# Random-feature attention into a gated MLP on one core: later planned DMA landings, a new set of plan seeds, and other places for the tails' x and P1

## The chip, the cores and the metric

The kernel runs on one core of one Trainium2 chip. The metric is the device time of one execution in microseconds (us), lower is better. The program is one launch; the host only lays the inputs out in another order. In the profile PE is TensorE's matmuls and PEld its weight loads, DVE is VectorE, ACT is ScalarE, POOL is GpSimd, and SP is SyncE, which here does nothing but issue DMAs.

## The reference

```python
def _attn_ref(q, k, v, omega):               # q, k, v: (8, 8, 576, 64), omega: (128, 64)
    scale = 1.0 / np.sqrt(np.sqrt(D))
    def phi(x):                              # of q * scale, k * scale
        proj = np.einsum('bhsd,md->bhsm', x, omega)
        h = proj - np.sum(x * x, axis=-1, keepdims=True) / 2.0
        return np.exp(h - np.max(h, axis=-1, keepdims=True)) / np.sqrt(m)
    kv = np.einsum('bhsm,bhsd->bhmd', k_p, v)
    z = np.sum(k_p, axis=2)
    num = np.einsum('bhsm,bhmd->bhsd', q_p, kv)
    den = np.einsum('bhsm,bhm->bhs', q_p, z)[..., None] + 1e-06
    return num / den
def _moe_ref(x, w_a, w_b, w_out):            # x: (4608, 512); 512 -> 1536 -> 512
    return ((x @ w_a) * (x @ w_b)) @ w_out
```

The attention's output, heads side by side, is the x of the gated product. The q that is passed in is 3.366 times as large as the 0.1 of k and v. Weights arrive as 64-bit floats.

## The kernel before, in words

**Stages.** A *unit* u is a batch with a pair of heads, 32 in all (8 batches, 4 pairs). Attention of a unit: random features of k and q by one burst of TensorE, row maxima and biases on VectorE, exponentials on ScalarE, sums of k's features (z) on GpSimd and VectorE, k times v on TensorE, division by the denominators, a turn of q's features through DRAM, and the product that gives x. The 576 rows of a batch are 512 and a *tail* of 64; the tails of all batches are gathered in DRAM (xtd) and form a ninth batch of 512 rows, b = 8. The MLP runs over batches b = 0 to 8 in steps; `steps` holds the first matmul of each, 12 per batch. Every matmul of the MLP is made of three, with both operands split into a high and a low part.

**Seven products for eight.** Batches 0 and 1 (`moe_block`) multiply plainly. From batch 2 on (`moe_block7`) the products with w_a and w_b take a Strassen-like scheme: seven products per pair i of feature blocks and per weight w (0 is w_a, 1 is w_b), with sums of the weights (tiles t and bq) that are computed once, by `weight_sums`, stored in DRAM and loaded again for each batch. Batches 7 and 8 (`Out7`) do the same with w_out: `out_sums` makes the sums (tiles owr and otf, result ot). Of its seven products, P1 is computed into the bank p1 that the w_a and w_b products also use (`one` in `items`), and is copied by ScalarE the first time, later added by VectorE, into an oc tile. `ones7` is the list of P1 products that wait for their place in `unit`.

**Slots.** A tile lives in a slot of its ring (x0 to x3, raw0, raw1, and so on), or in one of the slots of other rings that its `more` list names. Tiles of the weight sums (wr, tf), outputs before their store (osb), and w_out's sums (owr) all use raw0 and raw1. The `LATE` lists name what the last two batches may take over from the attention.

**The planner.** The whole kernel is first recorded as a graph of operations, each with a cost in ns for the engines that can do it. `plan` simulates it: at each step every engine takes the operation that can start first, ties by priority. VectorE, ScalarE and GpSimd (`EDF`) go by due times instead, which `dues` works out backwards from TensorE's order of a first pass. The order thus found is then written out, and the engines keep it, whatever really happens: an operation that waits holds up everything behind it on its engine. DMAs are costed as their bytes at 330 bytes per ns, one after another, plus `LANDING`; a reader that is sensitive to late data has a `margin` or a `land` in addition. `slot_free` says from when a slot can be taken: the end of its last user and 70 ns (`LAT`).

`CHOSEN` holds one seed per slice of `STEP` ns. A seed other than 0 makes `shifted` add Gaussian noise to the due times of the operations due within `LOOK` of the slice's start. The kernel before has one tuple of 53 seeds and slices of 20,000 ns.

**Lines.** L417, L419 and L425 are the copies and differences that split into high and low parts. L428 is the issue of every DMA except those named apart. L594 and L611 are the attention's bursts, L651 and L652 the biases, L834 and L835 `groups`, L844 and L845 `total`, L889 and L890 `inv`. L884 is the denominators' row sum, L1073 the plain product with w_out, L1089 to L1096 `out_sums`, L1143 a product of `Out7`, L1263 and L1271 the plain MLP, L1294 to L1303 `weight_sums`, L1356 and L1366 a product of seven and the sum behind it, L1416 the gate's product.

Of the kernel before, what the change touches and what calls it, by code (L numbers as in the profile page):

```python
# [39 lines left out]

CFG = dict(PORT=0.5, EDF=("DVE", "ACT", "POOL"), ROUNDS=2, STEP=20000, LOOK=60000, TRIES=8, NOISE=(1000,), CHOSEN=((4,6,0,1,0,7,8,6,1,5,0,0,1,8,0,2,0,0,0,8,1,0,0,0,0,6,1,0,0,6,7,3,2,0,0,4,0,0,0,0,0,1,3,2,0,1,0,0,0,0,0,0,0),), TOOK=[], SAY=False, ZS=800, ZB=(1500, 3000, 5000), ZD=(1500, 3000, 4500), HQ=(2500, 4000, 5000), BACK2=(1500, 2500, 4000), TW=(), WAIT=150, RAW=2000, FAST=(0, 1, 2, 3), JOIN0=False, WARM=8, HROOM=["w0", "u1", "w1", "u2", "w2", "u3"], H=3, TURN=(7,), BACK=1500, AT=2, GATES=(-4, -1, 2, 5), SQPE=4, MARGIN=1200, LOAD=2500, SUMS=1000, NATS=(1, 2, 3), CONV=(28000, 2600))

# [16 lines left out]
class Graph:  # L59
    LAT = 70  # L60
    OVER = {"DVE": 78, "ACT": 100, "POOL": 40, "PE": 0, "SP": 0}
    ENGINES = ("PE", "ACT", "DVE", "POOL", "SP")
    BW, LANDING = 330.0, 2000

# [74 lines left out]
    def dues(self):  # L139
# [21 lines left out]
        while heap:  # L161
            d, _, o = heapq.heappop(heap)
            e = next(iter(o.eng))
            cost = o.end - o.start if o.bytes else o.eng[e]
            if e in CFG["EDF"]:
                now = min(-d, ptr.get(e, inf))
                if now < -d:
                    heapq.heappush(heap, (-now, -o.n, o))
                    continue
                ptr[e] = now - max(30, o.eng[e] - self.OVER[e])  # L170
            o.due = -d
            for n in before[o]:
                same = "PE" in o.eng and "PE" in n.eng
                late[n] = min(late[n], o.due - cost - o.margin - (0 if same else self.LAT + (150 if "PE" in n.eng else 0)))
# [52 lines left out]
    def run(self, until=1e12, due=None):  # L227

        free, ready, found = self.free, self.ready, {}
        while len(self.done) < len(self.ops):  # L230
            best = None
            for e in self.ENGINES:
                mine = None
                for o in ready[e]:
                    at = 0, ()
                    if o.alloc:
# [5 lines left out]
                        if not at or at[1] == ():  # L242
                            continue
                    s = max(free[e], o.need, at[0])
                    for x in o.eng:
                        if x != e and max(free[x], o.need, at[0]) + o.eng[x] <= s + o.eng[e] - (o.eng[e] <= o.eng[x]):
                            break
# [43 lines left out]

    def cost(self, since):

        at, c = since, 0
        for o in self.done:
            if "PE" in o.eng and o.end > since:
                gap = max(0, o.start - at)
                c += gap + 1600 * (gap > 1900)
                at = o.end
        return c  # L300

    def shifted(self, due, at, k):

        rnd = random.Random(k)
        near = [o.n for o in self.ops if o.end is None and o.due < at + CFG["LOOK"]]
        due = list(due)
        for n in near:
            due[n] += rnd.gauss(0, CFG["NOISE"][k % len(CFG["NOISE"])])
        return due

    def plan(self):

        self.begin()
        self.run()
        self.sort()
        self.dues()
        due, best, chosen = [o.due for o in self.ops], None, CFG["CHOSEN"]
        for turn in range(len(chosen) or CFG["ROUNDS"]):
            self.begin()
            at, now, took = 0, list(due), []  # L320
            while len(self.done) < len(self.ops):
                i = len(took)
                seeds = [chosen[turn][i]] if chosen else [0] + [1 + 1000 * turn + k for k in range(CFG["TRIES"])]
                if len(seeds) > 1:
                    kept, tried = self.keep(), []
                    for k in seeds:
                        self.run(at + CFG["LOOK"], self.shifted(now, at, k) if k else now)
                        tried.append((self.cost(at), k))
                        self.back(kept)
                    seeds = [min(tried)[1]]  # L330
                took.append(seeds[0])
                now = self.shifted(now, at, seeds[0]) if seeds[0] else now
                at += CFG["STEP"]
                self.run(at, now)
            self.sort()
            end = max(o.end for o in self.order)
            if chosen or best is None or end < best[0]:
                best = end, self.order, {o: (o.start, o.end, o.eng, [b.slot for b in o.alloc]) for o in self.ops}
                due = now
                CFG["TOOK"].append(took)  # L340
            if CFG["SAY"]:
                print(turn, end, flush=True)
        _, self.order, was = best
        for o in self.ops:
            o.start, o.end, o.eng, slots = was[o]
            for b, slot in zip(o.alloc, slots):
                b.slot = slot
        return self.order
# [28 lines left out]
def tile_attention_moe(ctx: ExitStack, tc: tile.TileContext, kqt, kqtt, kqn, kqnt, vx, omst, idn, wab, wout, out):  # L377
# [12 lines left out]
    for name, n in dict(X=2, Xw=0, nat=2, x2=0, v=2, hk=1, hq=2, qd=1, kvz=0, sm=3, sq=3, ht=3, Xt=1, xl=0, xts=2, rd=2, x=4, xa=2, xf=2, Sa=2, Sb=2, st=0,  # L390
# [6 lines left out]

    LATE = dict(wo=["hk0", "hq0"], ot=["X0", "X1", "hq1", "qd0"], owr=["raw0", "raw1"], og=["nat0", "nat1", "ht0", "ht1"], ogf=["xf0", "xf1"],
                oc=["v0", "v1", "Xt0", "raw0", "raw1"])
# [218 lines left out]
    def scores(nm, b, pri, x, xdep, dst, c0, sm, sq, flat, held, more):  # L618
# [29 lines left out]
        def biases(e):  # L648
# [3 lines left out]
            nc.vector.scalar_tensor_tensor(bi, s, -1.0, tm, op0=ALU.mult, op1=ALU.subtract)  # L652
        g.op({"DVE": 300}, biases, r=[(sm, (c0, 0)), (sm, (c0, 1)), (psq if sq is None else sq, None)], w=[(sm, (c0, 0)), (sm, (c0, 1))], prio=pri + 2)
        for w in range(2):
# [6 lines left out]
    ends = {}  # L661
    xstage = {}

    def pair(u, gate):
# [143 lines left out]
    def z_sums(u, pr, hk, mg):  # L808
# [27 lines left out]
        g.op({"DVE": 2 * dve(2 * M)}, groups, r=[(zs, None)], w=[(z2, None), (zq, 0)], alloc=[zq], prio=pri, margin=CFG["ZS"])  # L836

# [5 lines left out]
        def total(e):  # L843
            nc.vector.tensor_reduce(zw.ap[0:32, 0:8], zq.ap[0:32, 0:4].rearrange("p i c -> p c i"), axis=X, op=ALU.add)  # L844
            nc.vector.transpose(zx.ap[0:32], zw.ap[0:32])  # L845
        g.op({"DVE": 320}, total, r=[(zq, 0), (zq, 1)], w=[(zw, None), (zx, None)], alloc=[zx], prio=pri)
        g.op({"SP": 330}, dma(lambda: zd, lambda: zx.ap[0:8]), r=[(zx, None)], w=[(zd_b, None)], prio=-30, nbytes=32 * 8 * 4)
# [27 lines left out]
    def divide(u, pr, hq, zb):  # L875
# [15 lines left out]
        g.op({"DVE": 340}, inv, r=[(dn, None)], w=[(dn, None)], prio=pri)  # L891
        for c in range(NCH):
# [87 lines left out]
    def tok_tail(b, hp, nm, pr, mg, more, vb, h, xt):  # L980
# [47 lines left out]
        g.op({"PE": 4 * 108}, go, r=[(x32t, None), (ident, None)], w=[(px, None)], alloc=[px, *xt.new], prio=pr + 150, margin=mg)  # L1028
        split(b, hp, lambda: px.ap[:], (px, None), pr + 150)
# [54 lines left out]
    def out_sums(i, wo, ot, gate=()):  # L1084
# [3 lines left out]
        for k in range(2):  # L1088
            g.op({"DVE": dve(E)}, lambda e, k=k: nc.vector.tensor_tensor(wr.ap[:, k], f(wo[k].ap[:, 0]), f(wo[k].ap[:, 1]), op=ALU.add),  # L1089
                 r=[(wo[k], None)], w=[(wr, k)], alloc=[wr, tf] if k == 0 else [], prio=-7, deps=gate, land=2500)  # L1090
        b11, b12, b21, b22 = (lambda k=k, h=h: wr.ap[:, k, HM * h:HM * h + HM] for k in range(2) for h in range(2))
# [228 lines left out]
    def moe_block7(b):  # L1320
# [10 lines left out]
        def unit(i, w, C):  # L1331
# [120 lines left out]
    def attention(u, room=None):  # L1452

        gate = steps[-1:] if u >= 2 * NHP else []
        if u == KS:
# [15 lines left out]
    for b in range(B + 1):  # L1471
# [94 lines left out]
```

## Time and profile before

| what | value |
|---|---|
| median of three runs | 1061.02 us (1060.23 to 1061.48) |
| the profiled execution's own time | 1057.47 us |
| its span, first to last instruction | 1055.7 us |
| TensorE busy | 1039.7 us, 7806 matmuls |
| VectorE, ScalarE, GpSimd busy | 885.0, 597.3, 111.1 us |
| moved by DMA | 314.16 MB, 298 GB/s on the mean |
| DMAs issued on SP | t 168 and wo 96 of 512 KB, bq 84 of 256 KB, and others |

Durations below come from the one profiled execution. A group's row gives line, engine, operation, out<-in with buffer numbers left out, shapes, count, then busy time in us, mean ns of one, and the engine's idle time before such instructions with what ended it. A piece of the timeline gives start, length, engine, line, operation and tiles, and in brackets idle time and what ended it. Who ended a wait is inferred from semaphores.

### The profile page before, as it was taken

Reading aid. Unit: us, or ns where it says so; the run is one execution under the profiler, and the core shown is the slowest. Engines: PE = TensorE matmul, PEld = TensorE weight load, DVE = VectorE, ACT = ScalarE, POOL = GpSimd, SP = SyncE. Lnnn points to the kernel's source line nnn. Section 1 sums busy time; section 2 is a strip of 40 time slices with the busy share of each in tenths; the row PEclk is TensorE's granted clock in tenths of the full one; section 3 lists DMA queues with packets and bytes.
Section 4 is the critical chain, followed back from the end, with each engine's and each line's share of the span. In section 5 each row is a group of like instructions: output and inputs, shape, how many; then the busy total and the mean of one; then the engine's idle time right before and its main releaser. Section 6 shows DMA issues by size and latency. Waiting matters only on the chain. (4 is left out here: it accounts for less than half of the span.)

```text
span 1055.7 us, 22026 instructions
## 1 busy us (share of the span) xinstructions
PE 1039.7 (98%) x7806; PEld 915.4 (87%) x7806; DVE 885.0 (84%) x2218; ACT 597.3 (57%) x1650; POOL 111.1 (11%) x177
## 2 busy tenths in 40 slices
PE   9999999999999999999999999999999999999998
PEld 8877777777788888888888898988899898999998
DVE  6999999799988788888886978778876658998866
ACT  8998887666665655665564656564564213233211
POOL 0021111111111111111020111111110000000000
PEclk9999999999999999999999999999999999999999
DMA  9886877899899989988889888988887878899991
GB/s 354 315 249 224 308 258 248 279 356 340 267 334 350 311 300 300 334 312 296 297 291 353 299 297 290 360 290 292 272 287 261 277 255 294 317 373 341 364 310 47
DMA packets 123646, 314.16 MB, mean 298 GB/s; under 512 B 17680, under 2 KB 40976, under 8 KB 123536
## 3 DMA queue, kind: packets, MB, share of 16 engines
q1 hardware_dynamic: 122656, 312.10, 85.7%
q8 instruction: 61, 1.00, 0.4%
q10 hardware_dynamic: 880, 0.66, 0.2%
q14 instruction: 49, 0.40, 0.1%
HBM read 255.52 MB, written 57.18 MB: 296 GB/s over the span
## 5 line engine op out<-in xcount | busy, mean ns | idle before, releaser
L1366 DVE TENSOR_TENSOR c<-p,c 128x512 f32<-128x512 f32 (+1 forms) x336 | 207.4, 617 | 83.1 <-PE p L1356 70.4
L1073 PE MATMUL o<-wo,ghl 128*128 128x512 f32 x1008 | 258.7, 397 | 3.1 <-DVE ghl L425 2.2
L1073 PEld LDWEIGHTS o<-wo,ghl 128*128 128x128 f32 x1008 | 181.0, 188 | 42.7 <-DVE ghl L425 3.9
L1356 PE MATMUL p<-Sa,t 128*128 128x256 f32 x1008 | 134.9, 283 | 0.0
L1356 PEld LDWEIGHTS p<-Sa,t 128*128 128x128 f32 x1008 | 126.4, 189 | 0.4
L818 POOL TENSOR_TENSOR z<-hk 128x256 f32<-128x256 f32 x56 | 44.6, 797 | 653.6 <-ACT hk L657 417.9
L417 ACT CAST ghl<-c 128x512 fp32r<-128x512 f32 (+1 forms) x71 | 39.9, 576 | 101.3 <-DVE c L1416 90.6
L894 ACT ACTIVATE hq<-hq,dn 128x128 f32<-128x128 f32 x224 | 71.4, 393 | 29.9 <-DVE dn L890 28.3
L417 ACT COPY c<-p 128x256 f32<-128x256 f32 x84 | 31.1, 370 | 96.8 <-PE p L1356 91.7
L884 DVE CUSTOM_DVE_ANT_0 zero<-hq,zb 128x128 bf16<-128x128 f32 x224 | 76.0, 339 | 1.5 <-DMA zb<-zdr 0.5
L1263 PE MATMUL pa<-x,wa 128*128 128x512 f32 x288 | 74.6, 400 | 0.8 <-ACT a L417 0.7
L1356 PE MATMUL p<-x,t 128*128 128x256 f32 x504 | 73.8, 282 | 1.3 <-ACT oc L417 0.7
L1263 PE MATMUL pb<-x,wb 128*128 128x512 f32 x288 | 73.4, 398 | 1.3 <-DVE a L1271 1.3
L1356 PE MATMUL p<-Sb,t 128*128 128x256 f32 x504 | 74.3, 283 | 0.0
L1356 PE MATMUL p<-Sb,bq 128*128 128x256 f32 x504 | 73.8, 282 | 0.4 <-DMA bq<-bd 0.4
L1356 PEld LDWEIGHTS p<-x,wa 128*128 128x128 f32 x504 | 65.1, 188 | 6.5 <-DVE c L1366 3.9
L1356 PE MATMUL p<-x,wa 128*128 128x256 f32 x504 | 68.9, 283 | 1.6 <-DVE c L1366 1.6
L1356 PE MATMUL p<-x,wb 128*128 128x256 f32 x504 | 68.7, 282 | 0.4 <-DVE c L1366 0.2
L1356 PEld LDWEIGHTS p<-x,t 128*128 128x128 f32 x504 | 65.8, 188 | 3.2 <-DVE c L1366 1.5
L1356 PEld LDWEIGHTS p<-x,wb 128*128 128x128 f32 x504 | 65.0, 188 | 4.0 <-DVE c L1366 1.3
L1356 PEld LDWEIGHTS p<-Sb,t 128*128 128x128 f32 x504 | 66.2, 189 | 0.8 <-ACT c L417 0.4
L1356 PEld LDWEIGHTS p<-Sb,bq 128*128 128x128 f32 x504 | 65.8, 189 | 0.7 <-DMA bq<-bd 0.6
(202 smaller groups left out, 2032.4 us busy)
## 6 DMA issues: line engine op xcount, KB each, us to landing
t<-td SPq DMA_DIRECT2D x168, 512.0 KB
wo<-wod SPq DMA_DIRECT2D x96, 512.0 KB
bq<-bd SPq DMA_DIRECT2D x84, 256.0 KB
qdr<-qd SPq DMA_DIRECT2D x112, 160.0 KB
hq<-qdr SPq DMA_DIRECT2D x28, 640.0 KB
X<-in_kqt_dram SPq DMA_DIRECT2D x30, 512.0 KB
raw<-in_wab_dram SPq DMA_DIRECT2D x24, 512.0 KB
td<-ts SPq DMA_DIRECT2D x24, 512.0 KB
```

The costliest lines, as they stand in the source:

```text
L417: nc.scalar.copy(o(), i())
L818: g.op({"POOL": pool2(n)}, lambda e: nc.gpsimd.tensor_tensor(o(), a(), c(), op=ALU.add), r=r, w=w, alloc=list(al), prio=pri, deps=zload[-1 ...
L884: g.op({"DVE": 413}, lambda e, c=c, j=j, rr=rr, qc=qc: nc.vector.tensor_tensor_reduce(out=junk.ap[rr], in0=qc(), in1=zb.ap[rr, j], scale=1 ...
L894: g.op({"ACT": 392}, lambda e, c=c, src=src: nc.scalar.activation(hq.ap[:, c], src(), AF.Copy, scale=dn.ap[:, c:c + 1]), r=[sd, (dn, None) ...
L1073: nc.tensor.matmul(po.ap[:], ghl.ap[:, gi, t * P:(t + 1) * P], wo.ap[:, wi], start=(n == 0 and i == 0), stop=(n == NF - 1 and i == 2))
L1263: nc.tensor.matmul(pb.ap[:], wt.ap[:, wi, c], xs[c].at(xi), start=(c == 0 and i == 0), stop=(c == NC4 - 1 and i == 2))
L1356: nc.tensor.matmul(pb.ap[:, half], wcol(wi, c), xc(xi, c), start=n == 0, stop=n == 5)
L1366: g.op({"DVE": dve(n)}, lambda e: nc.vector.tensor_tensor(c4.ap[:, o], pb.ap[:, half], y(), op=ALU.add), r=[*((pb, k) for k in range(half. ...
```

## The change

- **Landings.** `LANDING` goes from 2000 to 3400. Margins that had covered late data shrink: `RAW` 2000 to 600, `LOAD` 2500 to 1100, w_out's `land` 2500 to 1100, `ZB`, `ZD`, `HQ`, `BACK2` by 1200 to 1400 at each stage. `SAFE`, 500, is new: it is added to the readers of a DMA that have neither `land` nor `margin`, and to the time at which a slot is free if a DMA was among its users. `dues` counts both as well.
- **Prices.** `biases` 300 to 379 ns, `groups` 60 more, `total` 320 to 423, `inv` 340 to 416.
- **Seeds.** One tuple of 70 seeds with slices of 15,000 ns. Noise is 300 ns for even seeds and 1000 for odd ones; an odd seed also holds two fifths of the attention's TensorE operations that are near back by up to `HOLD`, 1000 ns. The search for seeds is taken out of `plan`; `LOOK` stays.
- **Places.** xl, the tails' x as it comes back from DRAM, gets the slots v0, v1, Xt0 and hq0. `owr` gets its list from `CFG`.
- **Order.** With `ONE=((7, 1),)` P1 of batch 7, pair 1, is put in the unit of w = 1; all others stay at w = 0. `TG=1` gates each part of `weight_sums` one step earlier. `turned[CFG["G4"]:]` with `G4=4` gates the first unit of the second batch.

```diff
-    BW, LANDING = 330.0, 2000
+    BW, LANDING = 330.0, 3400
...
-            t = max(t, o.end + self.LAT)
+            t = max(t, o.end + self.LAT + (CFG["SAFE"] if o.bytes else 0))
...
-            t = max(t, d.start + 1, d.end + (0 if same else self.LAT + (150 if "PE" in d.eng else 0)) + (o.land if d.bytes else 0) - (900 if d in o.late else 0))
+            t = max(t, d.start + 1, d.end + (0 if same else self.LAT + (150 if "PE" in d.eng else 0)) + (o.land or CFG["SAFE"] * (not o.margin) if d.bytes else 0) - (900 if d in o.late else 0))
...
-                    s = max(free[e], o.need, at[0])
+                    need = o.need if due is None else o.need + due[len(self.ops) + o.n]
+                    s = max(free[e], need, at[0])
...
+        for o in near:
+            due[o.n] += rnd.gauss(0, CFG["NOISE"][k % len(CFG["NOISE"])])
+        if k % 2:
+            for o in near:
+                if "PE" in o.eng and 0 <= o.prio < 10 ** 6 and rnd.random() < 0.4:
+                    due[len(self.ops) + o.n] = rnd.random() * CFG["HOLD"]
...
+        for seeds in CFG["CHOSEN"]:
+            self.sort()
+            self.dues()
+            now = [o.due for o in self.ops] + [0] * len(self.ops)
+            self.begin()
+            for i, k in enumerate(seeds):
+                now = self.shifted(now, i * CFG["STEP"], k) if k else now
+                self.run((i + 1) * CFG["STEP"], now)
+            self.run(1e12, now)
...
-            if ones7 and w == 0:
+            if ones7 and w == ((b, i) in CFG['ONE']):
...
-        gate = steps[-1:] if u >= 2 * NHP else []
+        gate = steps[-1:] if u >= 2 * NHP else turned[CFG["G4"]:] if u == NHP else []
...
-                    xl = g.buf("xl", [P, SM], F32, f"xl{hp}", ["X0", "X1", "hk0", "hq0", "hq1"])
+                    xl = g.buf("xl", [P, SM], F32, f"xl{hp}", CFG["XL"])
...
-                weight_sums(k // 2, k % 2, [steps[NF * b + k]])
+                weight_sums(k // 2, k % 2, [steps[NF * b + k - CFG["TG"]]])
```

More of the change, by code (lines that the diff above doesn't have):

```diff
@@ L39 @@
 KS = NHP
-CFG = dict(PORT=0.5, EDF=("DVE", "ACT", "POOL"), ROUNDS=2, STEP=20000, LOOK=60000, TRIES=8, NOISE=(1000,), CHOSEN=((4,6,0,1,0,7,8,6,1,5,0,0,1,8,0,2,0,0,0,8,1,0,0,0,0,6,1,0,0,6,7,3,2,0,0,4,0,0,0,0,0,1,3,2,0,1,0,0,0,0,0,0,0),), TOOK=[], SAY=False, ZS=800, ZB=(1500, 3000, 5000), ZD=(1500, 3000, 4500), HQ=(2500, 4000, 5000), BACK2=(1500, 2500, 4000), TW=(), WAIT=150, RAW=2000, FAST=(0, 1, 2, 3), JOIN0=False, WARM=8, HROOM=["w0", "u1", "w1", "u2", "w2", "u3"], H=3, TURN=(7,), BACK=1500, AT=2, GATES=(-4, -1, 2, 5), SQPE=4, MARGIN=1200, LOAD=2500, SUMS=1000, NATS=(1, 2, 3), CONV=(28000, 2600))
+CFG = dict(PORT=0.5, EDF=("DVE", "ACT", "POOL"), STEP=15000, LOOK=60000, NOISE=(300, 1000), CHOSEN=((140892,0,232461,659925,412462,880754,0,848445,0,0,175606,0,728814,0,0,0,560286,0,0,0,0,0,0,0,0,0,0,0,0,0,0,0,0,0,0,0,0,0,0,0,0,0,0,0,0,0,0,0,0,0,0,0,0,0,0,0,0,0,545343,0,0,0,0,0,0,0,0,0,0,0),), ZS=800, ZB=(300, 1600, 3600), ZD=(300, 1600, 3100), HQ=(1100, 2600, 3600), BACK2=(300, 1100, 2600), TW=(), XL=["v0", "v1", "Xt0", "hq0"], OWR=["raw0", "raw1"], ONE=((7, 1),), SAFE=500, HOLD=1000, TG=1, G4=4, WAIT=150, RAW=600, FAST=(0, 1, 2, 3), JOIN0=False, WARM=8, HROOM=["w0", "u1", "w1", "u2", "w2", "u3"], H=3, TURN=(7,), BACK=1500, AT=2, GATES=(-4, -1, 2, 5), SQPE=4, MARGIN=1200, LOAD=1100, SUMS=1000, NATS=(1, 2, 3), CONV=(28000, 2600))
 class Buf:
@@ L173, in dues @@
                 same = "PE" in o.eng and "PE" in n.eng
-                late[n] = min(late[n], o.due - cost - o.margin - (0 if same else self.LAT + (150 if "PE" in n.eng else 0)))
+                late[n] = min(late[n], o.due - cost - o.margin - (o.land or CFG["SAFE"] * (not o.margin) if n.bytes else 0) - (0 if same else self.LAT + (150 if "PE" in n.eng else 0)))
                 left[n] -= 1
@@ L290, in sort @@
         self.order = sorted(self.done, key=lambda o: (o.start, o.n))
[L292 to L300, printed above, removed]
     def shifted(self, due, at, k):
         rnd = random.Random(k)
-        near = [o.n for o in self.ops if o.end is None and o.due < at + CFG["LOOK"]]
+        near = [o for o in self.ops if o.end is None and o.due < at + CFG["LOOK"]]
         due = list(due)
-        for n in near:
-            due[n] += rnd.gauss(0, CFG["NOISE"][k % len(CFG["NOISE"])])
+        for o in near:
[4 more added lines that the diff above has]
+                    due[len(self.ops) + o.n] = rnd.random() * CFG["HOLD"]
         return due
@@ L314, in plan @@
         self.run()
-        self.sort()
[L316 to L347, printed above, removed]
+        for seeds in CFG["CHOSEN"]:
[7 more added lines that the diff above has]
+            self.run(1e12, now)
+        self.sort()
         return self.order
@@ L396, in tile_attention_moe @@
                 tst=["Sa0", "Sb0", *(f"u{k}" for k in range(NF))], bq=["a0", "a1"], osb=["raw0", "raw1"])
-    LATE = dict(wo=["hk0", "hq0"], ot=["X0", "X1", "hq1", "qd0"], owr=["raw0", "raw1"], og=["nat0", "nat1", "ht0", "ht1"], ogf=["xf0", "xf1"],
+    LATE = dict(wo=["hk0", "hq0"], ot=["X0", "X1", "hq1", "qd0"], owr=CFG["OWR"], og=["nat0", "nat1", "ht0", "ht1"], ogf=["xf0", "xf1"],
                 oc=["v0", "v1", "Xt0", "raw0", "raw1"])
@@ L652, in biases @@
             nc.vector.scalar_tensor_tensor(bi, s, -1.0, tm, op0=ALU.mult, op1=ALU.subtract)
-        g.op({"DVE": 300}, biases, r=[(sm, (c0, 0)), (sm, (c0, 1)), (psq if sq is None else sq, None)], w=[(sm, (c0, 0)), (sm, (c0, 1))], prio=pri + 2)
+        g.op({"DVE": 379}, biases, r=[(sm, (c0, 0)), (sm, (c0, 1)), (psq if sq is None else sq, None)], w=[(sm, (c0, 0)), (sm, (c0, 1))], prio=pri + 2)
         for w in range(2):
@@ L662, in tile_attention_moe @@
     xstage = {}
+    turned = []
     def pair(u, gate):
@@ L835, in groups @@
             nc.vector.tensor_reduce(zq.ap[:, 0], flat(z2).rearrange("p (c r) -> p c r", r=32), axis=X, op=ALU.add)
-        g.op({"DVE": 2 * dve(2 * M)}, groups, r=[(zs, None)], w=[(z2, None), (zq, 0)], alloc=[zq], prio=pri, margin=CFG["ZS"])
+        g.op({"DVE": 2 * dve(2 * M) + 60}, groups, r=[(zs, None)], w=[(z2, None), (zq, 0)], alloc=[zq], prio=pri, margin=CFG["ZS"])
         def shift(e):
@@ L890, in inv @@
             nc.vector.reciprocal(dn.ap[:], dn.ap[:])
-        g.op({"DVE": 340}, inv, r=[(dn, None)], w=[(dn, None)], prio=pri)
+        g.op({"DVE": 416}, inv, r=[(dn, None)], w=[(dn, None)], prio=pri)
         for c in range(NCH):
@@ L1027, in go @@
                 nc.tensor.transpose(px.ap[:, c * P:(c + 1) * P], x32t.ap[:, c].rearrange("p j d -> p (j d)"), ident.ap[:])
[L1028 removed]
+        turned.append(g.op({"PE": 4 * 108}, go, r=[(x32t, None), (ident, None)], w=[(px, None)], alloc=[px, *xt.new], prio=pr + 150, margin=mg))
         split(b, hp, lambda: px.ap[:], (px, None), pr + 150)
```

6 lines of the change are left out of this document (3 added, 3 removed).

## The prediction

> **What bounds the kernel now.** I read the page's first section first, then TensorE's busy time by stretches of the span, then the single pieces around each stretch where it idles.
>
> ```profile
> span 1055.7 us, 22026 instructions
> PE 1039.7 (98%) x7806; PEld 915.4 (87%) x7806; DVE 885.0 (84%) x2218; ACT 597.3 (57%) x1650; POOL 111.1 (11%) x177
> ```
>
> TensorE works 1039.7 of 1055.7 us. The change removes no matmul, so it can only act on the 16.0 us of idle time. The next view gives that idle time by stretch: length, TensorE busy (instructions), granted clock, DMA share, GB/s.
>
> ```profile
> 0.00:1.00 1.00, 0.01 (x1) 1.00 0.00 0
> 1.00:36.00 35.00, 35.00 (x332) 1.00 0.99 380
> 36.00:105.00 69.00, 66.96 (x406) 1.00 0.75 243
> 105.00:225.00 120.00, 118.62 (x729) 1.00 0.85 287
> 225.00:330.00 105.00, 103.19 (x663) 1.00 0.90 313
> 330.00:879.00 549.00, 547.01 (x4282) 1.00 0.88 301
> 879.00:892.00 13.00, 10.59 (x79) 1.00 0.95 307
> 892.00:1051.00 159.00, 158.30 (x1328) 1.00 0.82 295
> 1051.00:1055.70 4.70, 0.00 (x0) 0.96 0.59 181
> ```
>
> The reader is to see that the first 0.99 us (nothing to do yet) and the last 4.70 us (the last sum and its store) belong to any order of this work. The rest, 16.0 - 0.99 - 4.70 = 10.3 us, is stalls: 2.04 at 36 to 105, 1.39 to 225, 1.81 to 330, 1.99 in the 549 us to 879, 2.41 at 879 to 892, 0.70 after. The granted clock is 1.00 where matmuls run, so nothing is to be had there.
>
> Two of the stretches have one cause. Pieces are start, length, engine, line, operation, tiles, count, and in brackets idle time and what ended it. First the one to 225, rows of SP, VectorE and TensorE:
>
> ```profile
> 205.46 0.40 SPq L428 DMA_DIRECT2D out_dram<-osb  x1
> ...
> 211.55 1.03 DVE L1303 TENSOR_TENSOR tf<-wr 128x512 f32<-128x512 f32 x1 [3.65 <-DMA out_dram<-osb]
> ...
> 221.34 0.69 DVE L425 TENSOR_TENSOR ghl<-a,ghl 128x512 fp32r<-128x512 f32 x1
> ...
> 222.08 1.20 PE L1073 MATMUL o<-wo,ghl 128*128 128x512 f32 x4 [1.38 <-DVE ghl L425]
> ```
>
> osb (an output on its way out) and tf (a temporary of the weight sums) share the two raw slots. VectorE, which works in its written order, stood 3.65 us at 211.55 until a store of 256 KB had landed, 6.0 us after the last store's issue at the least. The plan of before counts 262144/330 = 0.79 us of transfer plus 2.0 of landing plus 0.07, so 2.87. VectorE then ran late, and TensorE paid 1.38 us for ghl. Of the 3.65, then, 3.65 - 1.38 = 2.27 had been slack.
>
> Then 879 to 892; the first line is from the chain of waits (start, length, what):
>
> ```profile
> 880.06 6.29 DMA out_dram<-osb
> ...
> 886.48 0.69 DVE L1093 TENSOR_TENSOR otf<-owr 128x512 f32<-128x512 f32 x1 [0.47 <-DMA out_dram<-osb]
> ...
> 881.02 0.58 ACT L417 COPY oc<-p 128x512 f32<-128x512 f32 x1 [1.44 <-PE p L1143]
> ...
> 881.66 0.98 PE L1356 MATMUL p<-x,t 128*128 128x256 f32 x6 [0.68 <-ACT oc L417]
> ...
> 887.82 0.95 PE L1356 MATMUL p<-x,t 128*128 128x256 f32 x6 [0.50 <-DVE c L1366]
> ...
> 891.30 0.87 PE L1143 MATMUL o_P<-ot,ghl 128*128 128x256 f32 x5 [1.00 <-DVE ot L425]
> ```
>
> Again a store, 6.29 us against 2.87 planned, holds the raw slot that otf (w_out's sums) wants. The chain runs from it through otf, c and ot to two stalls, 0.50 and 1.00 us. The third, 0.68 us, is another matter: P1 (the first product of w_out's seven) sits in a bank that the next product needs, and ScalarE's 0.58 us copy stands between.
>
> **The change part by part.** The sum is made against the profiled execution, 1057.47 us (its span of 1055.7 and 1.8 around it). The median of the runs is 1061.02, which is 3.5 above; I carry the difference over to the median unchanged.
>
> *Landings.* LANDING goes from 2000 to 3400 ns, and six margins (RAW, LOAD, ZB, ZD, HQ, BACK2) and w_out's land give back 1400 each (the first of ZB, ZD, HQ, BACK2 1200 to 1400). So a load that has such a margin is planned as before, or 0.2 us later. What shifts is the rest. X and v, whose MARGIN stays, are planned 1.4 us later. The readers of t, bq and wo are planned 1.4 + 0.5 (SAFE) = 1.9 us later, and so is the moment when a slot comes free that a store has read. No instruction is added, and the chip's landings stay what they are; SP issues in plan order. The value is in the order: the planner puts something else where it now expects tf and otf. At 211.55 the surprise falls from 3.65 to 1.75 us, below the slack of 2.27, so term **A is -1.4 us** (bounds 0, if tf keeps its place, and -1.4). At 880 the store is expected after 4.77 us instead of 2.87, and two owr sums, each as wide as otf's 0.69, go before otf, so the surprise of 6.29 is nearly covered: term **B is -1.5 us**, the 0.50 and the 1.00 (bounds 0 and -1.5). Of TensorE's own waits, one is on a load:
>
> ```profile
> 305.15 0.97 PE L1356 MATMUL p<-Sb,bq 128*128 128x256 f32 x6 [0.43 <-DMA bq<-bd]
> ```
>
> So the loads arrive ahead of their use, and that lead hides a later plan: cost nothing. Where the lead is under 1.9 us, the planner puts a filler product (o or o_P) ahead of a load that is already there; this too costs nothing while fillers are left, and up to 1.9 us at a place where none is.
>
> The Trainium skill speaks against this part: the page "DMA: Bandwidth & Descriptors" (section "Anatomy of one DMA") puts a DMA at a nearly constant 2.0 us plus its bytes over 436 GB/s, so by estimate 2.6 us for 256 KB, which is what the old plan holds. It fits the path from GpSimd; here SP issues, and the 6.0 and 6.29 us above disagree with it. By that figure A and B would be nothing (the first rival below).
>
> *VectorE's prices.* Biases go from 300 to 379 ns, total from 320 to 423, groups up 60, inv up 76.
>
> ```profile
> L651 DVE SCALAR_TENSOR_TENSOR sm<-sm,sq 128x8 f32<-128x8 f32 x61 | 10.0, 164 | 0.3
> L652 DVE SCALAR_TENSOR_TENSOR sm<-sq,sm 128x8 f32<-128x8 f32 x61 | 10.4, 170 | 2.1
> ...
> L844 DVE TENSOR_REDUCE zw<-zq 32x8 f32<-32x32 f32 x28 | 5.3, 189 | 1.1 <-ACT zq L840 1.0
> L845 DVE STREAM_TRANSPOSE zx<-zw 32x32 f32<-32x32 f32 x28 | 5.6, 200 | 1.0
> ...
> 55.97 1.19 PE L1263 MATMUL pb<-x,wb 128*128 128x512 f32 x4 [1.26 <-DVE a L1271]
> ```
>
> 164 + 170 is 334 and 189 + 200 is 389, without the gap between two dependent operations, so the old prices were below what ran and the new ones a little above. With 68 biases (61 and 7 of the ends) the plan missed at most 68 x 79 + 28 x (103 + 60 + 76) = 12.1 us of VectorE over the span, most of it hidden while VectorE has spare time. The same stretch with all engines (TensorE, its loads, VectorE, ScalarE, GpSimd) shows where there is none:
>
> ```profile
> 36.00:105.00 69.00, 66.96 (x406) 52.68 (x404) 67.26 (x168) 62.94 (x162) 14.03 (x18) 1.00 0.75 243
> ```
>
> VectorE works 67.26 of 69 us, so errors add up: some six biases between 36 and 55.97 are 6 x 79 = 0.5 us. **C is -0.5 us** (bounds 0 and the whole 1.26).
>
> *Tails' x.* xl moves from X0, X1, hk0, hq0, hq1 to v0, v1, Xt0, hq0; ot (X0, X1, hq1, qd0) gets room, and oc (v0, v1, Xt0, raw0, raw1) loses three of its five. *P1 in batch 7, pair 1* moves from w = 0 to w = 1.
>
> ```profile
> L425 DVE TENSOR_TENSOR x<-xl,x x4: 414/546/682, 891.8 to 916.8; 128x256 fp32r<-128x256 f32 x2, 128x512 fp32r<-128x512 f32 x2
> ```
>
> The 0.68 us at 881.66 leaves that place. The next product into that bank is then today's at 887.82; with 0.58 us for the copy, P1's copy is due at about 887. But its oc tile now needs a slot that xl holds until its sums are read, in today's order up to 916.8, while raw0 and raw1 are owr's. VectorE must bring such a tile's last two readers (0.41 for a half width and 0.68 for a whole one, 1.1 us) forward, ahead of c and ot. Bounds: -0.68, and +2.7 if a whole pair of tails (four sums of half width and one whole, 2.3 us, and 0.4 of hand-overs) goes first. I take nothing: today's 0.68 comes back half a step on.
>
> *Gates.* weight_sums may start one step sooner (TG). The sums also wait for the raw slots, which are what is scarce there, so I take nothing, between 0 and the 1.81 us of 225 to 330. Three of the words have no counterpart in the diff: OWR repeats the list that stood there; G4=4 gates the second batch on turned[4:], which is empty, as only four units have appended to it; LOOK stays 60000. Cost 0.
>
> *Seeds.* 10 of 70 slices of 15 us have a seed, against 24 of 53 slices of 20 us, so the times at which the planner's orders are shaken change everywhere. The other 5.3 us of stalls (10.3 - 1.4 - 2.4 - 1.3, rounded) are thus drawn anew; I expect them unchanged, bounds -5.3 and +3.
>
> Sum: -1.4 - 1.5 - 0.5 = -3.4: span 1052.3, profiled time 1054.1, median 1061.0 - 3.4 = **1057.6**.
>
> **The rivals.** *No change, 1061* (0.25): landings are not what the plan gets wrong, or the stalls only move. Then A and B are nothing, C leaves 1060.5, and the stalls that are drawn anew blur it by 2 us either way. For it: landings of 6.0 us and more still exceed the 4.77 now planned. Against: one cause stands behind both stretches, and the plan moves the right way. The page of the Trainium skill named above speaks for this one.
>
> *Slower, 1064* (0.21): the slot for P1. For it: the readers of xl stand as late as 916.8, and P1 is due at 887; VectorE is 84% busy. Against: the planner sees this wait. Price: TensorE waits 2.7 us for P1's bank, ot comes 2.3 us later behind the same work, and B's 1.5 us stay, so 5.0 - 1.4 - 0.5 = +3.1: 1064.1. It decides from a P1 copy about 3.4 us late; below that the gains win.
>
> *Most stalls go, 1053.5* (0.11): better prices and landings also clear 225 to 330 and two thirds of the rest, -3.4 - 1.8 - 2.3 = -7.5. Against are stalls like the following, behind VectorE work that no edit prices or moves.
>
> ```profile
> 418.66 0.73 PE L1073 MATMUL o<-wo,ghl 128*128 128x512 f32 x2 [0.55 <-DVE ghl L425]
> ```
>
> The floor is 1061.0 - 10.3 = 1050.7.
>
> **How the numbers follow.** The forecast, 1055 to 1059, has 0.43. A change under 0.2%, 2.1 us, can't be told from none here. Faster is 0.43 + 0.11 = 0.54, the same 0.25, slower 0.21. The range runs from 1053.0, past the middle of the best case, to 1064.0, near the price of the slot; about 0.07 lies below and 0.11 above.
>
> **What would show it.** A: no wait of VectorE over 2.3 us on out_dram<-osb, and no stall on ghl behind one. B: under 1 us idle in the 13 us around the first w_out sums, and a short otf wait. C: no 1.26 us stall before pb in the first 105 us. P1: its ScalarE copy half a step later, and TensorE's wait there under 1 us. TensorE's idle time should be about 12.6 us. It is wrong if idle time stays at 16 with the stalls elsewhere, or if a wait for a slot of oc or x shows on the chain.

## The result, and the profile after

The changed kernel takes 1045.2 us (median of five, 1043.85 to 1045.67), against 1061.0 us before (now five runs, 1060.11 to 1061.51): 15.8 us less, a ratio of 0.985 with a 95% interval from 0.9836 to 0.9865. The forecast was 1057.6 with a range down to 1053.0, so it had the sign and missed the size by a factor of more than four. The profiled execution took 1044.68 us, 12.8 less than the one before.

The first rows of the page after (line numbers of the changed kernel are 27 or 28 lower than those of before):

```profile
span 1042.9 us, 22086 instructions
PE 1032.5 (99%) x7806; PEld 912.1 (87%) x7806; DVE 889.8 (85%) x2218; ACT 596.4 (57%) x1650; POOL 113.8 (11%) x177
```

TensorE's idle time fell from 16.0 to 10.4 us. But its *busy* time fell as well, from 1039.7 to 1032.5, with the same 7806 matmuls: 7.2 of the 12.8 us came out of time that the page counts as work. The same view by stretches as before (length, TensorE busy, clock, DMA share, GB/s):

```profile
36.00:105.00 69.00, 66.24 (x403) 1.00 0.75 251
105.00:225.00 120.00, 120.00 (x723) 1.00 0.87 295
225.00:330.00 105.00, 104.46 (x699) 1.00 0.91 315
330.00:879.00 549.00, 548.28 (x4322) 1.00 0.89 303
879.00:892.00 13.00, 13.00 (x112) 1.00 1.01 391
892.00:1038.20 146.20, 145.67 (x1227) 1.00 0.82 291
```

Idle time is 2.76 us in the first row (2.04 before), nothing to 225 (1.39 before), 0.54 to 330 (1.81), 0.72 to 879 (1.99), nothing in the 13 us where 2.41 had been, and 0.53 after. The waits of TensorE in all (engine, line, waited for: us, times, longest), the largest ones before:

```profile
PE p L1356 <- DVE c L1366: 2.4, 8, 0.5
PE o L1073 <- DVE ghl L425: 2.2, 3, 1.4
PE pb L1263 <- DVE a L1271: 1.3, 1, 1.3
PE o_P L1143 <- DVE ot L425: 1.0, 1, 1.0
```

And after:

```profile
PE px L1000 <- DVE x32t L989: 2.2, 2, 1.3
PE none L418 <- DVE zero L411: 1.0, 1, 1.0
PE p L1329 <- DVE c L1339: 0.8, 3, 0.3
PE pa L1236 <- DVE x L397: 0.6, 1, 0.6
PE o L1046 <- ACT ghl L389: 0.2, 1, 0.2
PE o L1046 <- DVE ghl L397: 0.2, 1, 0.2
```

Three of these four kinds (o behind ghl, pb behind a, o_P behind ot) are gone or down to 0.2 us behind VectorE. New are 2.2 us in the first 50 us, at px, a turn of the attention's x.

**Where the 7.2 us of busy time went.** I took the distance from each matmul's start to the next one's, and for each pair of kinds its median over all the kernels traced here. Distances over the median by 15% or more are late ones; pairs that are rare or whose median is under 0.11 us, as in the attention's bursts, are left out. Before there were 157, after 115; what they have above the median, less what the profile counts as idle, was 16.8 us before and 12.1 after. The typical late one is only 0.10 us above its median and shows no idle time. Most of those behind an idle gap have that gap and 0.16 us on top. In rows: before, six matmuls p<-Sb,bq behind a wait (at 305.15, shown in the prediction) last 0.97 us; six of the same kind with no wait ahead, after, last this long:

```profile
879.39 0.87 PE L1329 MATMUL p<-Sb,bq 128*128 128x256 f32 x6
```

So 4.7 of the 7.2 us are small stalls that a busy TensorE hides. 1.5 us are a slightly smaller usual spacing (118.8 to 118.1 ns in L1329's products). All other kernels traced here, old or new, have 118.1 to 118.3 ns, so this belongs to the one profiled execution of before and not to the change; its cause is open. The last 1.0 us is spread over bursts and changes between kinds.

### The profile page after: what moved, and what is told of

Read it like the earlier page. It is cut to its first block, busy times and chain, and to the rows that moved or that the text cites. A ratio compares the mean times of both kernels' runs of the same rounds, so it can differ in the third digit from the quotient of the medians.

```text
span 1042.9 us, 22086 instructions
## 1 busy us (share of the span) xinstructions
PE 1032.5 (99%) x7806; PEld 912.1 (87%) x7806; DVE 889.8 (85%) x2218; ACT 596.4 (57%) x1650; POOL 113.8 (11%) x177
## 4 chain that ended last, share of the span: by engine, by line
PE 94%; DVE 5%; ACT 1%; issue 1%; DVEq 0%; ACTq 0%
PE p L1329 39%; PE o L1046 22%; PE pa L1236 7%; PE pb L1236 6%; PE o_P L1116 5%; PE pkv L838 3%; PE ppk L566 3%; PE pm L906 2%; PE ppk L583 2%; PE p L583 1%; DVE c L1339 1%; PE p L1116 1%; PE ppke L566 1%; PE pkv L968 1%; DVE sm L616 1%
## 5 line engine op out<-in xcount | busy, mean ns | idle before, releaser
L1329 PE MATMUL p<-Sa,t 128*128 128x256 f32 x1008 | 133.9, 281 | 0.3 <-ACT c L389 0.2
L1329 PEld LDWEIGHTS p<-Sa,t 128*128 128x128 f32 x1008 | 124.9, 188 | 1.0 <-ACT c L389 0.7
L857 DVE CUSTOM_DVE_ANT_0 zero<-hq,zb 128x128 bf16<-128x128 f32 x224 | 80.5, 359 | 2.8 <-DVE dn L857 0.2
L1329 PE MATMUL p<-Sb,bq 128*128 128x256 f32 x504 | 74.1, 283 | 0.0
L1329 PE MATMUL p<-Sb,t 128*128 128x256 f32 x504 | 73.7, 282 | 0.0
L1329 PE MATMUL p<-x,t 128*128 128x256 f32 x504 | 73.4, 281 | 0.1
L1329 PEld LDWEIGHTS p<-x,wa 128*128 128x128 f32 x504 | 65.1, 188 | 4.8 <-DVE c L1339 2.1
L1329 PE MATMUL p<-x,wa 128*128 128x256 f32 x504 | 68.1, 282 | 0.7 <-DVE c L1339 0.6
L1329 PE MATMUL p<-x,wb 128*128 128x256 f32 x504 | 68.4, 282 | 0.2 <-DVE c L1339 0.2
L1329 PEld LDWEIGHTS p<-x,wb 128*128 128x128 f32 x504 | 64.5, 188 | 3.5 <-DVE c L1339 0.6
L1329 PEld LDWEIGHTS p<-Sb,bq 128*128 128x128 f32 x504 | 65.9, 189 | 0.5
L629 ACT ACTIVATE hq<-hq,sm 128x128 f32<-128x128 f32 x192 | 64.3, 393 | 2.9 <-DVE sm L624 2.9
L1329 PEld LDWEIGHTS p<-x,t 128*128 128x128 f32 x504 | 65.5, 189 | 0.5 <-DVE oc L1126 0.4
```

The costliest lines, as they stand in the source:

```text
L629: g.op({"ACT": 392}, lambda e, c=c, w=w, to=to, at=at: nc.scalar.activation(to.ap[:, at + c], src[w](c), AF.Exp, scale=SC, bias=sm.ap[:, 2 ...
L857: g.op({"DVE": 413}, lambda e, c=c, j=j, rr=rr, qc=qc: nc.vector.tensor_tensor_reduce(out=junk.ap[rr], in0=qc(), in1=zb.ap[rr, j], scale=1 ...
L1329: nc.tensor.matmul(pb.ap[:, half], wcol(wi, c), xc(xi, c), start=n == 0, stop=n == 5)
```

## The experiments

Each is timed beside the kernel before on the same chip. There it took 1059.0 to 1059.8 us (medians of 7 to 25 runs, from 1056.15 to 1063.8). The changed kernel itself was timed only beside the 1061.0, so its gain is 15.8 us there, and 14 if its 1045.2 held on the other chips. Since a seed acts on one plan only, most experiments have all seeds 0; four pairs repeat the question with two arbitrary draws of 70 even seeds (noise of 300 ns), called A and B.

| kernel | landings | prices | places, gates | seeds | median us | ratio, 95% interval | TensorE busy, idle | late matmuls |
|---|---|---|---|---|---|---|---|---|
| before | old | old | old | own | 1061.0 | | 1039.7, 16.0 | 157 |
| changed | new | new | new | own | 1045.2 | 0.9836 to 0.9865 | 1032.5, 10.4 | 115 |
| e1 | new | new | new | none | 1047.0 | 0.9875 to 0.9909 | 1032.4, 12.8 | 127 |
| e2 | old | old | old | none | 1051.6 | 0.9917 to 0.9946 | 1034.6, 14.9 | 139 |
| e3 | old | new | new | none | 1061.0 | 1.0005 to 1.0032 | 1038.9, 20.8 | 153 |
| e4 | new | new | old | none | 1051.6 | 0.9917 to 0.9948 | 1035.7, 16.3 | 153 |
| e5 | new | new | new | A | 1055.6 | 0.9953 to 0.9980 | 1034.2, 18.8 | 126 |
| e6 | old | new | new | A | 1058.2 | 0.9980 to 1.0001 | 1038.1, 18.6 | 154 |
| e7 | new | new | new | B | 1050.0 | 0.9893 to 0.9931 | 1035.7, 14.2 | 146 |
| e8 | old | new | new | B | 1056.3 | 0.9961 to 0.9985 | 1037.2, 17.1 | 167 |
| e9 | new | new | TG 0 | none | 1047.5 | 0.9874 to 0.9903 | 1032.7, 13.0 | 127 |
| e10 | new | new | old xl, P1 | none | 1050.5 | 0.9901 to 0.9937 | 1032.8, 16.2 | 133 |
| e11 | new | old | new | none | 1058.6 | 0.9984 to 1.0002 | 1039.3, 17.4 | 148 |
| e12 | new | old | old | none | 1061.9 | 1.0011 to 1.0037 | 1039.8, 21.3 | 159 |
| e13 | new | old | new | A | 1059.9 | 0.9994 to 1.0013 | 1038.4, 20.5 | 137 |
| e14 | new | old | new | B | 1055.1 | 0.9949 to 0.9977 | 1034.2, 18.2 | 135 |
| e15 | old | old | old | A | 1057.8 | 0.9970 to 0.9988 | 1039.8, 17.1 | 159 |
| e16 | old | old | old | B | 1063.1 | 1.0023 to 1.0043 | 1041.7, 23.2 | 180 |
| e17 | new | biases old | new | none | 1050.6 | 0.9901 to 0.9930 | 1034.7, 13.8 | 129 |
| e18 | new | biases new | new | none | 1052.0 | 0.9913 to 0.9946 | 1033.8, 15.1 | 133 |

**What the plan itself expects.** The planner in each kernel.py needs no chip. Run by itself, it gives the time at which it expects TensorE's last matmul to end; the median less that time is the *lag*, how far the chip is behind its plan. Only differences between kernels count, since the plan leaves out what follows the last matmul. Some 2 us of the lag with old landings are there from the first loads on, before any order matters.

| kernels | plan's last matmul ends, us | lag, us |
|---|---|---|
| before; changed | 1042.1; 1042.7 | 19.0; 2.5 |
| all new: e1, e5, e7 | 1047.7, 1052.1, 1047.7 | -0.7, 3.5, 2.3 |
| old landings: e3, e6, e8 | 1048.8, 1051.3, 1048.3 | 12.2, 7.0, 8.0 |
| old prices: e11, e13, e14 | 1053.1, 1051.9, 1051.3 | 5.5, 8.0, 3.7 |
| all old: e2, e15, e16 | 1046.1, 1050.2, 1048.8 | 5.5, 7.6, 14.3 |
| e4, e9, e10 | 1050.7, 1047.5, 1050.9 | 0.9, 0.1, -0.4 |
| e12 | 1054.6 | 7.3 |
| e17, e18 | 1049.4, 1049.0 | 1.2, 3.0 |

The changed kernel's plan is no shorter than that of before: its gain is that the chip keeps to the plan. The seven kernels with new landings and all new prices have lags of -0.7 to 3.5 us, the eleven with old landings or all four old prices 3.7 to 19.0. By the starts of single VectorE operations, the kernel before is behind its plan by 1.1 us at 5 us, 4.1 at 203, 7.1 at 345 and 8.7 at 1025; the changed one by -0.7 at 7, 0.3 at 210, -0.6 at 347 and -4.5 at 1026.

### Seeds, landings, places (e1 to e4)

My theory was that the later landings carry most of the gain. The rival was that the seeds do: an order is a draw, and these were good ones.

e1 and e2 set all seeds to 0, in the changed kernel and in the one before:

```diff
-CHOSEN=((140892,0,232461,659925,412462,880754,0,848445,...),)
+CHOSEN=((0,0,0,0,0,0,0,0,...),)
```

> The changed kernel with all 70 seeds set to 0: landings, prices, places and gates as changed, nothing shaken. If the planner's later landings carry the gain, it keeps most of the 15.8 us: 1045 to 1050. If the seeds carry it (a lucky draw, kept because it was good), the order without them is an ordinary one: 1055 to 1061.

> The kernel before with all 53 seeds set to 0. Landings theory: the old plan is poor with or without seeds, 1058 to 1066. Seeds theory: the old seeds were worth a few us too, so it gets slower than 1061 by 3 to 10 us: 1064 to 1071.

Without its seeds the changed kernel is at 1047.0, so they are worth 1.8 us by the medians, and 4.4 by the ratios to the kernel before, as the two ran on different chips. The kernel before gets *faster* by 7.7 us (1051.6 against 1059.3 on that chip). Neither theory expected this: its 24 seeds had been a loss on the chip, though in its plan they are a gain of 4.0 us. On these two alone, no more than 4.6 us are left for landings, prices and places together.

e3 puts the landings back in the changed kernel without seeds, e4 the places and gates:

```diff
-    BW, LANDING = 330.0, 3400
+    BW, LANDING = 330.0, 2000
-ZB=(300, 1600, 3600), ZD=(300, 1600, 3100), HQ=(1100, 2600, 3600), BACK2=(300, 1100, 2600)
+ZB=(1500, 3000, 5000), ZD=(1500, 3000, 4500), HQ=(2500, 4000, 5000), BACK2=(1500, 2500, 4000)
-SAFE=500 ... RAW=600 ... LOAD=1100 ... land=1100
+SAFE=0 ... RAW=2000 ... LOAD=2500 ... land=2500
```

```diff
-XL=["v0", "v1", "Xt0", "hq0"] ... ONE=((7, 1),) ... TG=1
+XL=["X0", "X1", "hk0", "hq0", "hq1"] ... ONE=() ... TG=0
```

> The changed kernel without seeds, with LANDING 2000, SAFE 0 and the old margins; prices, places and gates as changed. Landings theory: loses at least 6 us against the changed kernel without seeds, and VectorE waits again for stores out of the raw slots (over 2.3 us at once). Seeds theory: within 2 us of the changed kernel without seeds.

> The changed kernel without seeds, with xl in X0, X1, hk0, hq0, hq1, with all P1 at w = 0 and the weight sums gated as before (TG 0); landings and prices as changed. If the places carry the gain, it is over 4 us slower than the changed kernel without seeds, most of it around 880 to 892. By the prediction's step (nothing for the places) it is within 2 us.

The old landings cost 14.0 us, of which 12.9 are lag. The old places cost 4.6, of which 3.0 are a longer plan. In e3 ScalarE stands for DMAs (rows of its waits):

```profile
ACT natk L553 <- DMA natk<-in_kqn_dram: 8.0, 5, 3.2
ACT natq L553 <- DMA natq<-in_kqn_dram: 6.5, 5, 2.7
ACT ts L389 <- DMA td<-ts: 5.7, 3, 3.1
```

All such rows of ScalarE and VectorE add up to 35.7 us in e3, 15.0 in e1 and 20.2 in the changed kernel. The third row is new to me: a store of weight sums (td<-ts) is still reading the slot that ScalarE wants to fill. VectorE's wait for out_dram<-osb is 1.7 us and not the over 2.3 that I expected; 34.0 of the 35.7 us are ScalarE's. How much of that wait reaches TensorE, these rows do not show.

### Landings or the draw? (e5 to e8)

The same edit of the landings under two arbitrary draws:

```diff
+CHOSEN=((1000,1002,1004,...,1138),)     # A
+CHOSEN=((5000,5002,5004,...,5138),)     # B
```

> The changed kernel with 70 arbitrary seeds (even ones, noise of 300 ns), first draw. If an order's time is a matter of the draw, it lies anywhere from 1045 to 1062 whatever the landings; if the landings decide, it stays near the changed kernel without seeds (1047): 1044 to 1053.

> The same 70 arbitrary seeds with LANDING 2000, SAFE 0 and the old margins. Landings theory: slower than its partner with the new landings by 6 to 16 us, 1053 to 1064. Draw theory: as likely faster as slower than its partner.

> The changed kernel with a second draw of 70 arbitrary seeds. Landings theory: 1044 to 1053 again. Draw theory: over 5 us from the first draw.

> The second draw with LANDING 2000, SAFE 0 and the old margins. Landings theory: slower than its partner by 6 to 16 us, and ScalarE and VectorE together wait over 25 us for DMAs (15 us in the changed kernel without seeds, 36 with the old landings). Draw theory: no such difference.

With the new landings the three orders take 1047.0 (none), 1055.6 (A) and 1050.0 (B); with the old ones 1061.0, 1058.2 and 1056.3. The pairs differ by 14.0, 2.7 and 6.3 us, each with the same sign. A seed shakes every plan in its own way, so a pair is not matched draw for draw, and by chance three signs agree one time in four. But in lag the pairs differ by 12.9, 3.5 and 5.7 us, some 2 of them from the first loads, and their plans' ends only by 1.1, -0.8 and 0.6. So later landings help while the prices are new, and the draw alone moves the time by up to 8.6 us: both theories hold a part. A missed the landings theory twice, with 1055.6 (up to 1053 was allowed) and with its difference (6 to 16).

### Which of the places (e9, e10)

```diff
-TG=1
+TG=0
```

> The changed kernel without seeds, with only the gates of the weight sums as before (TG 0). The old places together cost 4.6 us (1051.6 against 1047.0). If it was the gates, 1050 to 1052 with new stalls between 105 and 330; if it was xl and P1, 1046 to 1048.

e10 has the first two places of e4's edit (xl and ONE) and keeps TG 1.

> The changed kernel without seeds, with only xl in its old slots and P1 at w = 0 (TG 1 stays). If xl and P1 carry what the places gain, the idle time at 879 to 892 comes back (1.7 us) and the time is 1049 to 1052; if they do not, 1046 to 1048. By the prediction's step it is the same within 0.7 us.

The gates are worth 0.5 us, xl and P1 3.5 us. In e10 the idle time sits where it was before, and 2.2 us more just ahead of it:

```profile
700.00:879.00 179.00, 176.80 (x1337) 1.00 0.85 275
879.00:892.00 13.00, 11.46 (x93) 1.00 0.88 299
```

That is 2.20 + 1.54 = 3.7 us idle, against 0.33 + 0.16 in e1. Two of its waits, for c and for oc, are the known ones; a third is for a load of w_out (the first row):

```profile
PE p L1116 <- DMA wo<-wod: 1.0, 1, 1.0
...
PE p L1329 <- ACT oc L389: 0.7, 1, 0.7
```

Here the cost is in the plan: it is e1's up to 850 us, and then has four waits of its own between 880 and 902, 3.2 us in all. In the changed kernel P1 comes half a step later, and two products stand between it and the next one that needs its bank. ScalarE's copy, then TensorE's pieces:

```profile
877.49 0.59 ACT L389 COPY oc<-p 128x512 f32<-128x512 f32 x1 [0.93 <-DVE c L1339]
```

```profile
877.25 0.88 PE L1116 MATMUL o_P<-ot,ghl 128*128 128x256 f32 x6
877.96 0.87 PE L1116 MATMUL o_P<-ot,og 128*128 128x256 f32 x6
878.67 0.88 PE L1329 MATMUL p<-x,t 128*128 128x256 f32 x6
```

The copy is done at 878.08, the bank is wanted at 878.67, and no wait is seen. Whether one of the two places would do alone was not tried: by the code, P1 at w = 0 with xl in the new slots takes a raw slot for the rest of the batch, and owr and otf, which need both, never get theirs. With P1 at w = 1 and xl in the old slots, the planner's last matmul ends at 1051.9, so the two are worth something together only.

### Prices (e11, e12)

```diff
-g.op({"DVE": 379}, biases ... 2 * dve(2 * M) + 60}, groups ... {"DVE": 423}, total ... {"DVE": 416}, inv
+g.op({"DVE": 300}, biases ... 2 * dve(2 * M)}, groups ... {"DVE": 320}, total ... {"DVE": 340}, inv
```

> The changed kernel without seeds, with the old prices of biases, groups, total and inv. By the prediction's step it loses 0.5 us (up to 1.3): 1047 to 1048.5. If a price that is 12 us short over the span matters as landings do, 1050 or more.

e12 is the kernel before without seeds (old prices and places) with only the landings new.

> The kernel before without seeds, with only the landings changed (LANDING 3400, SAFE 500, the smaller margins); old prices, places, gates. The kernel before without seeds took 1051.6. Landings theory, with the pairs seen so far (2.7, 6.3 and 14 us): 1045 to 1050, and ScalarE's and VectorE's waits for DMAs fall under 20 us from 24. Draw theory: 1047 to 1060, on either side.

Here my theory fell. The old prices cost 11.6 us, ten times what any expectation had, and the new landings on the old prices make the kernel before slower by 10.3 us (1061.9 against 1051.6), although ScalarE's and VectorE's waits for DMAs fall as expected, from 24.3 to 17.9 us. Fewer waits on DMAs are therefore not yet a faster kernel. Much of both losses is in the plans: e12's ends 8.5 us after e2's, e11's 5.4 after e1's, and only 1.8 and 6.2 us are more lag. In e11 the largest wait looks like VectorE's own lateness. These are TensorE's piece and VectorE's pieces ahead of it, with no gap from 246 on:

```profile
253.92 0.50 PE L1046 MATMUL o<-wo,ghl 128*128 128x512 f32 x1 [2.82 <-DVE ghl L397]
```

```profile
251.90 0.67 DVE L616 TENSOR_REDUCE sme<-htq 128x4 f32<-128x512 f32 x1
...
252.71 0.15 DVE L623 SCALAR_TENSOR_TENSOR sme<-sme,sqe 128x8 f32<-128x8 f32 x1
252.90 0.17 DVE L624 SCALAR_TENSOR_TENSOR sme<-sqe,sme 128x8 f32<-128x8 f32 x1
...
253.19 0.68 DVE L397 TENSOR_TENSOR ghl<-a,ghl 128x512 fp32r<-128x512 f32 x1
```

But e11's plan has this wait itself, 3.72 us long, behind the same row of VectorE operations without a gap. It is a poor place in the order, and not an operation that took longer than its price. No row here shows a wait that a short price causes.

### Prices or the draw? (e13 to e16)

The draws A and B again, with old prices alone, and with everything old:

> First draw of arbitrary seeds, new landings and places, old prices. With the new prices this draw took 1055.6. If the prices matter in themselves (without seeds they were worth 11.6 us), it is at least 3 us slower, 1058.5 to 1066; if that was the draw, 1050 to 1061 on either side.

> Second draw, new landings and places, old prices. With the new prices this draw took 1050.0. Prices theory: 1053 to 1062. Draw theory: 1046 to 1056 on either side.

> First draw with old landings, old prices and old places: the kernel before with other seeds. Without seeds it took 1051.6, with its own 1059. If both models are wrong by enough to cost, 1057 to 1065, and 1051.6 was luck; if the old plan is as good as the new, 1047 to 1056.

> Second draw with old landings, old prices and old places. Model theory: 1057 to 1065. Draw theory: 1047 to 1056.

The old prices cost 11.6, 4.3 and 5.1 us (none, A, B): the same sign each time. In lag it is 6.2, 4.5 and 1.4 us; the rest, 5.4, -0.2 and 3.6, is where the plans end, so a part of it is the draw. With everything old the three orders take 1051.6, 1057.8 and 1063.1. So 1051.6 was a lucky draw. The kernel's own seeds (1059 to 1061) give an ordinary time, but from the shortest plan of all and the largest lag.

Means over none, A and B: everything old 1057.5; old landings alone 1058.5; old prices alone 1057.9; all new 1050.9. By lag alone they are 9.1, 9.1, 5.7 and 1.7, and by the plans' ends 1048.4, 1049.5, 1052.1 and 1049.2. In these means, with either of the two wrong, nothing is left of what the other brings. Three draws that spread over 5 to 12 us don't prove it, "everything old" has the old places too, and 2.9 of the 7.0 us of the prices are longer plans. e1 and e2 alone misled: e2 is the luckiest of its three, and e4 at 1051.6 had lost the places.

### One price at a time (e17, e18)

e17 has only the price of biases old, e18 only those of groups, total and inv.

> The changed kernel without seeds, with only the price of biases old (300 instead of 379; 68 of them, 5.4 us of VectorE over the span). If the loss of 11.6 us goes by the VectorE time that the plan misses (5.4 of 12.1), about 1052; if it takes only one wrong price, as wrong as the others, to lose the whole, 1055 to 1061; if biases are harmless, 1046 to 1048.

> The changed kernel without seeds, with only groups, total and inv at their old prices (28 of each, 6.7 us of VectorE over the span). By the time that the plan misses, about 1053; one wrong price is enough, 1055 to 1061; harmless, 1046 to 1048.

The losses are 3.6 and 5.0 us, and 11.6 for all four prices. By the differences between the prices the plan misses 5.7, 6.7 and 12.4 us of VectorE (72 biases ran, not the 68 that I had counted). One wrong price is thus not enough for the whole loss. But 1.7, 1.3 and 5.4 of these losses are longer plans; in lag they are 1.9, 3.7 and 6.2, some 0.3 to 0.6 us for each us missed. This is one order each, and A and B put all four prices at 4.5 and 1.4 of lag.

## Why the prediction was wrong, point by point

**"It can only act on the 16.0 us of idle time", floor 1050.7.** This step failed first. 7.2 of the 12.8 us between the two profiled executions lay in busy time, and over the 20 kernels busy time ranges from 1032.4 to 1041.7 us with the same 7806 matmuls. The two ends of it are e1 and e16:

```profile
PE 1032.4 (99%) x7806; PEld 912.7 (87%) x7806; DVE 888.3 (85%) x2217; ACT 597.6 (57%) x1651; POOL 110.4 (11%) x177
```

```profile
PE 1041.7 (98%) x7806; PEld 915.0 (86%) x7806; DVE 887.2 (83%) x2219; ACT 596.2 (56%) x1649; POOL 109.4 (10%) x177
```

Busy time goes with the number of late matmuls, 127 and 180. The Trainium skill warns of this measure on the page "Trainium Kernel Development and Optimization" (section "Best Practices"): matmul busy share is not what the distance to the roofline is judged by. The traces here agree that it misleads, with 9.3 us between two kernels that do the same matmuls.

**The median carried over unchanged.** Wrong by 3.0 us. The profiled execution before was 3.5 us faster than its median, the one after 0.5. In one comparison the kernel before ran from 1056.15 to 1063.8 (13 runs), so one execution can well lie that far off.

**Landings, A and B, -2.9 us.** The direction was right, and so were both places: in the changed kernel VectorE waits for no out_dram<-osb, o stands behind ghl for 0.2 us on either engine, and the 13 us from 879 have no idle time. ScalarE has one wait of 3.2 us for such a store. The 2.87 us that the plan was said to hold was misread, though: the planner lines transfers up one behind another, and the plan of before gives these two stores 4.58 and 4.25 us. The size was wrong as well: 14.0, 2.7 and 6.3 us in three orders. I had priced two episodes; e3 shows many more, on ScalarE, which I had not looked at. The rival by which landings are worth nothing has the pairs against it as long as the prices are right.

**VectorE's prices, C, -0.5 us.** The worst-sized term: 11.6, 4.3 and 5.1 us, of which 6.2, 4.5 and 1.4 are lag and the rest where the plans end. The step that failed is "most of it hidden while VectorE has spare time": in lag, about half of the 12.4 us missed came through without seeds. By which waits is open. That the 12.1 us of the prediction lie close to the 11.6 us lost is chance, since 5.4 of those are a longer plan. That the order itself changes with a price had no term at all.

**Places, nothing.** Wrong by 3.5 us for xl and P1, in one order; right for the gates (0.5 us). The slot that the slower rival feared was never waited for. The planner ran the tails' sums as soon as their step allowed, where before they stretched from 884.7 to 916.8:

```profile
L397 DVE TENSOR_TENSOR x<-xl,x x4: 416/548/683, 874.8 to 880.0; 128x256 fp32r<-128x256 f32 x2, 128x512 fp32r<-128x512 f32 x2
```

"Today's 0.68 comes back half a step on" failed as well: fillers cover the copy. The rest of the 3.5 us is the load of w_out and the stretch ahead of 879, which I had not tied to xl's slots; the planner shows 3.2 us of it before any run.

**Seeds, unchanged.** Wrong on both sides: the old seeds are 7.7 us worse than none, the new ones 1.8 us better (4.4 by the ratios). Against the mean of the three draws, the old seeds lose 1.8 us (1059.3 against 1057.5) and the new ones gain 5.7 (1045.2 against 1050.9); the plan in between is worth 6.6. These three add up to 14.1 us, the difference to 1059.3. With three draws that spread over 9 to 12 us, the split is rough. Both sets of seeds shorten their plans, by 4.0 and 5.0 us. On the chip the old ones fall 19.0 us behind where 5.5 is the lag without them, the new ones 2.5 where it is -0.7. One set each does not show that the wrong landings and prices are why the old gain was lost, but it fits.

## What to carry to other kernels

Where a planner writes the order of engines that keep it, its prices are a part of the kernel: measure every operation that it places, DMA landings and short vector operations too, before searching for orders, because in the means here one wrong kind of price took back what the other had won. A tuned order is one draw; compare parameters over several draws, not by one pair. Set the planner's own end beside the measured time: it tells a poor plan, which needs no chip to see, from a chip that falls behind a good one. And judge what is left on TensorE by the distances between starts, since matmuls that come 0.1 us late count as busy.

## What the runs showed of the hardware that was not expected

Late matmuls cost without an idle gap: a distance over the usual one is most often 0.10 us long, there are 115 to 180 of them in a run, and 12 to 21 us of busy time lie in them. Nearly all that show no idle time have a weight load that starts late: in 132 of 135 before and in all 106 after it begins 0.04 us or more, mostly 0.107, after the start of the matmul ahead, where the usual is 0.002. Of these late matmuls 49 and 47 neither wait for a semaphore nor follow one that does; 75 and 52 follow a matmul that waits for one, and there the two kernels differ. Why the load is late is open. Stores of 256 KB issued by SP landed 6.0 and 6.3 us after issue, while the DMA engines moved 261 and 322 GB/s. A plan with still later landings was not run.
